# Constant-tile matmuls at the start of TensorE's queue, and a re-annealed plan, in a long-convolution plus linear-attention kernel

## The chip, the core and the metric

The kernel runs on one core of one Trainium2 chip. The time is the device time of one execution, in microseconds (us). Six engines or queues are named: PE (TensorE matmul; PEld is its weight load), DVE (VectorE), ACT (ScalarE), POOL (GpSimd), SP (SyncE, which here only issues DMAs) and the 16 DMA engines. Times in the profile count from the span's start.

## The reference

Two independent blocks over 2048 positions and 576 channels; their outputs stand side by side in the last axis.

```python
def _A_ref(q, k, v, shift_k, ssm_k, ssm_D):
    # k_shift: causal 4-tap convolution of k along S, a weight per channel and tap
    kv = k_shift * v
    # long causal convolution of kv with ssm_k along S, by FFT of length 2S
    y = irfft(rfft(pad(kv)) * rfft(pad(ssm_k)))[:S]
    return q * (y + kv * ssm_D)

def _B_ref(x, wqkv, wo):              # 32 heads of 18 channels
    q, k, v = split(x @ wqkv)
    pq, pk = phi(q), phi(k)           # phi(t) = t+1 if t > 0 else exp(t), plus 1e-6
    kv = einsum("hsd,hse->hde", pk, v); z = pk.sum(s)
    o = einsum("hqd,hde->hqe", pq, kv) / (pq . z + 1e-6)
    return o @ wo
```

## The kernel before

Every piece of work is an operation with a number: `P.op` (and `load` for DMAs) notes what it reads and writes, and gives for each engine that may do it a cost estimate. Nothing is issued there. A long string, `PLAN`, gives the order of issue and the engine of each operation (`P` PE, `A` ACT, `D` DVE, `G` POOL, `S` SP, then the number), and `PLACES` gives each buffer's byte offset in SBUF or its bank in PSUM. Both were made offline by an annealing planner from the estimates. At the end, `order = _issue(P)` reads the plan, and one loop allocates each buffer at its place and calls the operation's function. Each engine takes its operations strictly in the plan's order, waiting for data and for buffers on semaphores. SP issues all DMAs, in the plan's order, into one queue.

The work, by the names used below, with its lines:

- hs: six pieces of `ssm_k` (384 KB each) are loaded, transposed on PE in groups of eight (L480, "htr"), copied from PSUM to hT by ACT or DVE ("hev"), and one row gets `ssm_D` added (L489, "hD").
- Wj: PE spreads the shift weights over all partitions with matmuls that contract over one row (L412), ACT copies them (L415).
- x: `x_sb` holds x by rows. Half of the columns' transposes are done on PE (L343, "xtr", "xtrt"), half by transposing DMAs (L317, L329). Three of these tiles' names are xT, xTt and x_sb.
- k projection (L654, 10 matmuls of 288 columns), exponential on ACT (L659), phi on DVE (L662), 16 times. q projection (L675, 10 matmuls of 512), L679, L682, 10 times, into pqT.
- Convolution taps on DVE (L447 products, L452 and L455 sums), in six pieces; the product with v on DVE or POOL (L458). "Tap 72" below is operation 72, a product of the third piece.
- First transform stage on PE (L510, table Gsb), copied to Ch or Cu; then turned by a transposing DMA (L525) or by DVE (L536); second stage (L554, L561), copied to sph or spu; products p1 and p2 with the filter's spectrum (L595, L592) on DVE or POOL, after a row swap by DMA (X); first inverse stage (L603), copied to Vt; second inverse stage (L628, table Esb), and the product with q (L633).
- Attention: G = x'pk (L708, five groups of 32 matmuls), small products kv, z, den and M, the reciprocal (L795), stored to DRAM and read back spread over partitions (bct), pqT normalised (L838), output matmuls (L851), copies to ob, stores.

The first operations on PE are in the plan before: htr 289, Wj 10, htr 281, htr 287, xtr 46, htr 283, Wj 12, xtr 36, 32, 42, xtrt 34, 48, 38, L510 294 and 296, k 110. SP's first are: hs, cst (the table with the identity), shift weights, hs, x, D, x, x, Gsb, x, Gsb, the two wk loads, then kh (the rows of k), Gsb, kh, kh, the two wq loads, v, kh.

The diff touches the issue loop, a constant tuple beside the plan's other settings, and the two strings.

Of the kernel before, what the change touches and what calls it, by code (L numbers as in the profile page):

```python
# [103 lines left out]
def _issue(P):  # L104

    names = dict(P="PE", A="ACT", D="DVE", G="POOL", S="SP")
    order = []
    for w in PLAN.split():
        o = P.ops[int(w[1:])]
        o.eng = names[w[0]]  # L110
        order.append(o)
    places = [int(w) for w in PLACES.split()]
    for b, p in zip([b for b in P.bufs if b.space != "dram"], places, strict=True):
        b.pos = p
    assert sorted(o.id for o in order) == list(range(len(P.ops)))
    return order
# [99 lines left out]
def kernel(  # L216
# [13 lines left out]
    nc = tc.nc  # L230
# [50 lines left out]
    pqT = SB("pqT", [128, 5, S], side=1, pre=True)  # L281
# [246 lines left out]
    def s2(C, cc, pp, nm, bias):  # L528
        nw = PCH // 2
        g = cc * NPP + pp  # L530
        qt = nm == "u" and g not in UT
        if qt:
# [12 lines left out]
        for kp in range(2):  # L545
# [19 lines left out]
            def ev(e, kp=kp, ps=ps):  # L565
# [3 lines left out]
                else:  # L569
                    copy(e, sp.t[:].rearrange("p (r b) k -> p r b k", r=2)[:, :, 4 * kp:4 * kp + 4],  # L570
                         ps.t.rearrange("p r (b k) -> p r b k", b=4))
            aft = [seq[x] for x in (nm, ("h", g)) if x in seq] if kp == 0 else []
            last = P.op(("PE", T8), mm, rd=[ct, cst], wr=[ps], use=[sp], name="s2" + nm, bias=bias, cnt=8 if qt else 4,
                        after=aft)
# [301 lines left out]

    order = _issue(P)
    psall = nc.alloc_psum_tensor("ps_all", [128, 8, 512], FP32).ap()
    with tc.manual_schedule():
        cnt = 0  # L880
        for o in order:
            for b in o.bufs:
                if b.t is None and b.space != "dram":
                    if b.space == "ps":
                        b.t = psall[:, b.pos:b.pos + b.banks, :]
                    else:
                        cnt += 1
                        b.t = nc.alloc_sbuf_tensor_at("%s_%d" % (b.name, cnt), b.shape, b.dt, offset=b.pos)
            o.fn(o.eng)


T8 = 0.26
UT = (4, 6, 8)
XP = 2
BCD = 1
AFTER = dict(x=8, w=12, q=[3, 7])

PLAN = """
G9 S286 G14 S6 S8 G3 G5 S280 G30 S25 G1 S60 G0 G91 S22 G4 S23 G31 S57 P289 G2 S24 P10 S58 S41 P281 A11 P287 S40
P46 D288 A282 S15 P283 D290 A47 S59 P12 G285 D291 D284 S17 P36 A13 P32 S16 D33 A37 P42 S52 P34 P48 P38 P294 D35  # L900
S53 A49 D39 D43 S21 A295 P296 D297 S50 P110 S56 S28 P44 P298 A111 P101 D112 A299 S55 P92 D61 A45 P98 A93 D62 S54
P119 A99 A102 D94 D100 S18 P122 S20 D63 A120 S19 D64 P125 A123 D103 G65 D124 P107 A126 D121 P116 A108 D127 S51
D109 S321 D66 P292 A117 P128 A293 G29 S315 D67 P104 A129 D118 S300 P113 D130 P152 A114 A105 D115 P95 S305 A153
D68 P155 A96 S310 D106 D69 P161 A156 D97 S356 D72 S350 P158 A162 D154 D157 P137 A159 D163 S26 G70 P149 D160 A138
S27 P140 D139 A150 S7 D151 P322 A141 D71 P324 A323 P146 A325 D142 G326 P303 A147 P301 D73 P131 A304 A302 P134
D74 A132 S398 P316 D148 A135 P318 D133 A317 P308 D75 P143 A309 D136 G320 A319 P311 D77 P306 A144 P164 A307 D145
A312 D76 G185 S186 P333 A165 S189 P167 S399 A334 S188 D166 S187 D78 P327 A168 P329 A328 D169 D79 A330 P391 D82
P331 P170 A332 D80 D81 A392 S345 D83 S340 P387 A171 A172 P385 D84 S335 P182 A386 D85 D87 A388 S411 S412 D86 P389
A183 D88 P176 A390 D89 D184 G90 D393 P194 D177 P394 D195 P396 D406 A395 P196 A397 D178 P351 D197 D198 G400 P179
A352 D199 S210 P432 D180 D355 D419 S211 P173 D181 D401 D433 P438 S228 D174 D175 P479 S222 A439 P357 S224 D480  # L910
P359 S226 A358 P436 S218 G361 D360 A437 P409 S212 P313 D410 P353 S230 A314 P434 S214 D354 D223 P362 S424 A435
S220 P407 D229 A408 S453 P481 D225 A363 P191 G414 D440 S216 A482 P366 S425 D193 D192 A367 D466 P368 P338 A369
D339 P364 D231 A365 P485 P404 D413 A486 S375 P483 D405 A484 P402 S370 D227 P200 A403 P420 P336 D201 A421 S380
P208 D337 P348 A209 P343 P443 A349 D344 P417 S487 A444 P202 D418 P206 A203 P204 S445 A207 P422 S513 D205 P346
A423 P441 D219 P415 A442 P256 D347 G427 A416 P378 S472 A257 P341 S471 D379 P274 A342 S446 S258 D500 P454 S459
A275 P383 P381 A455 D384 P271 A382 D426 P373 P456 A272 P262 D217 A374 S273 S458 A457 P430 D215 A263 P376 P467
D221 S276 A431 P259 S264 D213 A377 P265 A468 S505 D260 P503 G447 S506 A266 P371 P516 A504 D372 P244 A517 S492
P490 P469 S519 A245 D491 P235 S493 S261 D470 P247 S518 A236 S246 D461 S190 P501 A248 P514 P488 S526 D448 A502
P428 S267 A489 P250 D460 S249 A429 D507 P238 S237 A515 D251 P464 A239 S252 D521 P451 S547 A465 P449 D495 P462
D520 A450 P253 A463 D494 P232 A254 D508 A452 P498 D474 A233 P511 S234 D499 S240 P509 A512 D473 P539 P542 D510  # L920
S255 P522 D543 P544 A523 P477 D545 P475 S546 D478 P537 A476 D540 P524 D538 P527 A525 S541 P529 D528 P496 D530
P534 S531 A497 P532 P554 D533 D535 P548 D555 S536 P268 D549 S556 P551 A269 S270 P557 D552 S550 P277 D558 S553
P241 D278 S559 S279 A242 S243
"""
PLACES = """
228384 226464 226432 218240 220192 33536 16512 143552 212480 206720 148160 149312 188256 167776 16768 52480
103040 35840 42240 1 2 20864 68864 1 0 0 3 1 3 7 2 78080 111232 90752 46336 136832 81152 192000 98944 6 33536 4
33536 2 39936 4 34688 2 39936 4 33536 6 33536 0 41088 6 109184 0 107136 6 109184 2 39936 4 33536 2 34688 0 39936
6 50432 2 39936 2 33536 6 33536 0 107136 6 50432 0 107136 4 33536 2 39936 4 39936 6 33536 206720 20608 6 6 4 4 6
50432 212480 32928 32928 68480 6 0 0 33248 78080 80128 6 6 0 2 4 43168 16512 34208 41120 18560 34976 37024 39072  # L930
32928 78080 2 18816 2 32928 0 21120 4 18816 0 18816 6 34080 4 19968 0 16512 6 32928 2 16512 2 58624 0 17664 6
16512 0 41504 0 40352 2 17664 38144 5 1 16768 6 0 56576 0 4 0 0 124544 107136 4 0 51584 124544 0 6 16512 46336 6
6 46336 4 5 120448 4 5 56192 0 3 3 0 24736 161600 0 6 20640 86272 4 2 103040 36256 4 6 132736 6 0 128640 6 7
128640 0 0 0 3 60288 24704 4 6 78080 28832 6 2 24736 115328 2 4 33536 3 0 0 0 56192 60288 6 2 120448 4 6 64384
60288 6 1 28832 0 4 56192 82176 2 6 140928 6 0 87296 0 3 3 3 145024 90368 2 0 98560 2 4 64384 102656 6 4 111232
6 6 50432 64384 4 4 54528 0 4 149312 0 3 0 3 94464 41504 0 6 59776 4 6 20608 78336 4 6 74240 2 4 107136 119424 2
2 123520 0 4 151360 6 2 2 6 2 6 4 2 143168 0 4 4 6
"""


# [28 lines left out]
```

## Time and profile before

| | |
|---|---|
| median of 8 runs | 177.06 us (176.18 to 177.67) |
| the profiled execution | 177.14 us, of which the span from first to last instruction is 175.3 us |
| PE busy | 157.4 us, 90% of the span, 1588 matmuls |
| PEld busy | 118.0 us |
| DVE busy | 147.7 us, 84%, 143 instructions |
| ACT busy | 111.5 us, 64%, 119 instructions |
| POOL busy | 36.0 us |
| DMA | 37.71 MB, mean 215 GB/s |

[...]The row that the profile calls PEclk is the clock that the throttle granted; whether the matmuls ran at that rate has to be read from their spacing. In the timeline a line gives the start, how long the merged group took, the engine, the line of code, the operation with output and inputs, the count, and in brackets how long the engine had been idle and what ended that.

### The profile page before, as it was taken

What the parts mean: (1) busy time and instruction counts of PE and PEld (TensorE: products, weight loads), DVE (VectorE), ACT (ScalarE), POOL (GpSimd) and SP (SyncE); (2) the same over time, 40 slices, a digit from 0 to 9 for tenths busy, and PEclk for the clock granted to TensorE, in tenths of its full rate; (3) what the DMA queues carried; (4) which work ended last, traced back from release to release, by engine and by line L of the source; (5) the groups of instructions that cost most, each with busy time, mean ns of one, the idle gap of its engine ahead of it and who ended that gap; (6) DMA issues with size and microseconds to landing.
All of it is one profiled execution on the core that took longest, in us unless ns stands there. A gap on an engine that the chain in (4) does not pass through costs nothing.

```text
span 175.3 us, 3813 instructions
## 1 busy us (share of the span) xinstructions
PE 157.4 (90%) x1588; PEld 118.0 (67%) x1588; DVE 147.7 (84%) x143; ACT 111.5 (64%) x119; POOL 36.0 (21%) x28
## 2 busy tenths in 40 slices
PE   0798999999969999699999997789999999999991
PEld 0577776767647766588768866655665679987770
DVE  0034599998999999999999999999898899998780
ACT  2362575576548899766360299999999697734211
POOL 8400003600702020000375005400901700000000
PEclk9999999999999999999999999999999999999999
DMA  6999999999999128079300178999998999954374
GB/s 151 288 325 326 371 342 175 220 380 236 242 274 320 65 52 311 4 137 211 135 0 14 50 245 254 167 209 150 220 246 329 374 324 326 329 156 152 120 238 137
DMA packets 53423, 37.71 MB, mean 215 GB/s; under 512 B 32991, under 2 KB 49501, under 8 KB 52894
## 3 DMA queue, kind: packets, MB, share of 16 engines
q1 hardware_dynamic: 53406, 37.47, 79.6%
q8 instruction: 12, 0.20, 0.5%
q14 instruction: 5, 0.04, 0.1%
HBM read 20.16 MB, written 4.98 MB: 143 GB/s over the span
## 4 chain that ended last, share of the span: by engine, by line
PE 55%; DVE 20%; ACT 15%; issue 4%; DMA 3%; SPq 1%; ACTq 0%; DVEq 0%
PE ps_all L851 12%; PE ps_all L603 8%; DVE m L447 7%; PE ps_all L654 7%; PE ps_all L675 6%; PE ps_all L628 6%; PE ps_all L708 5%; ACT Ch L254 4%; DVE m L452 4%; ACT Cu L254 3%; PE ps_all L510 3%; DMA hs<-in_A_ssm_k_dram 3%; ACT sph L254 3%; DVE pqT L682 3%; PE ps_all L343 3%
## 5 line engine op out<-in xcount | busy, mean ns | idle before, releaser
L447 DVE TENSOR_TENSOR m<-kh,Wj 128x3072 bf16<-128x3072 bf16 x12 | 23.2, 1955 | 0.0
L654 PE MATMUL ps_all<-wk,xT 128*128 128x288 bf16 x128 | 20.3, 290 | 2.1 <-DVE pk L662 1.8
L510 PEld LDWEIGHTS <-Gsb 128*128 128x128 bf16 x240 | 17.4, 102 | 6.4 <-issue 5.2
L851 PE MATMUL ps_all<-M,pqT 126*128 126x288 bf16 (+1 forms) x160 | 21.6, 286 | 0.0
L254 ACT ACTIVATE Cu<-ps_all 128x1536 bf16<-128x1536 f32 x10 | 15.3, 1559 | 9.6 <-PE ps_all L510 9.6
L675 PE MATMUL ps_all<-xT,wq 128*126 128x512 bf16 (+1 forms) x80 | 20.6, 380 | 0.0
L708 PE MATMUL ps_all<-pk,x_sb 128*128 128x288 bf16 (+1 forms) x160 | 20.6, 286 | 0.0
L458 POOL TENSOR_TENSOR v<-m,v 128x1536 bf16<-128x1536 bf16 x3 | 9.3, 3098 | 53.4 <-DVE m L455 53.4
L851 PEld LDWEIGHTS <-pqT 126*128 126x128 bf16 (+1 forms) x160 | 15.0, 97 | 5.8 <-issue 2.1
L675 PEld LDWEIGHTS <-wq 128*126 128x126 bf16 (+1 forms) x100 | 13.0, 131 | 7.8 <-issue 0.3
L708 PEld LDWEIGHTS <-x_sb 128*128 128x128 bf16 x160 | 15.5, 98 | 3.9
L254 ACT ACTIVATE Vt<-ps_all 128x1024 bf16<-128x1024 f32 x13 | 13.4, 1040 | 7.2 <-PE ps_all L603 6.3
L603 PE MATMUL ps_all<-cst,sph 128*128 128x128 bf16 x144 | 17.4, 219 | 0.4 <-ACT Cu L254 0.4
L254 ACT ACTIVATE spu<-ps_all 128x1024 bf16<-128x1024 f32 x15 | 15.3, 1046 | 3.7 <-PE ps_all L554 3.7
L254 ACT ACTIVATE Ch<-ps_all 128x1536 bf16<-128x1536 f32 x11 | 16.3, 1525 | 2.0 <-PE ps_all L510 2.0
L603 PE MATMUL ps_all<-cst,X 128*128 128x128 bf16 x144 | 17.4, 219 | 0.0
L654 PEld LDWEIGHTS <-xT 128*128 128x128 bf16 x128 | 12.6, 99 | 6.6 <-issue 3.1
L659 ACT ACTIVATE ek<-ps_all,neg 128x576 bf16<-128x576 f32 x16 | 11.6, 742 | 8.2 <-PE ps_all L654 8.1
L679 ACT ACTIVATE eq<-ps_all,neg 126x1024 bf16<-126x1024 f32 (+1 forms) x10 | 11.1, 1113 | 8.4 <-PE ps_all L675 8.4
L254 ACT ACTIVATE ob<-ps_all 128x576 bf16<-128x576 f32 x13 | 8.6, 659 | 10.3 <-PE ps_all L851 8.8
L603 PEld LDWEIGHTS <-sph 128*128 128x128 bf16 x144 | 14.0, 98 | 1.3 <-issue 0.9
L603 PEld LDWEIGHTS <-X 128*128 128x128 bf16 x144 | 14.1, 98 | 0.9 <-issue 0.5
(86 smaller groups left out, 295.1 us busy)
## 6 DMA issues: line engine op xcount, KB each, us to landing
X<-sph SPq DMA_DIRECT2D x18, 256.0 KB
hs<-in_A_ssm_k_dram SPq DMA_DIRECT2D x6, 384.0 KB
v<-in_A_v_dram SPq DMA_DIRECT2D x2, 1152.0 KB
out_dram<-ob SPq DMA_DIRECT2D x16, 144.0 KB
bct<-rden_rows SPq DMA_DIRECT2D x8, 252.0 KB
kh<-in_A_k_dram SPq DMA_DIRECT2D x1, 1584.0 KB
q<-in_A_q_dram SPq DMA_DIRECT2D x1, 1280.0 KB
out_dram<-q SPq DMA_DIRECT2D x4, 320.0 KB
```

What stands on the lines that cost most here:

```text
L254: nc.scalar.activation(out=o, in_=i, func=ACTF.Copy)
L447: nc.vector.tensor_tensor(out=m.t[:, i:i + 2], in0=i0, in1=i1, op=ALU.mult)
L458: lambda e: vec(e).tensor_tensor(out=vt.t[:, :, c0:c0 + CC], in0=m.t[:, 0], in1=vt.t[:, :, c0:c0 + CC], op=ALU.mult),
L510: nc.tensor.matmul(ps.t[:, bank, lo - 512 * bank:hi - 512 * bank], lhsT=Gsb.t[:, ri, bg, j, :], rhs=src[:, lo - CC * j:hi - CC * j], start ...
L603: nc.tensor.matmul(ps.t[:, j // 4, 128 * (j % 4):128 * (j % 4) + 128], lhsT=src.t[:, 8 * jp + j, :], rhs=W3(wi), start=(wi == 0), stop=(wi ...
L628: nc.tensor.matmul(o, lhsT=Esb.t[:, b, ri, :], rhs=vt[:, 2 * b + ri], start=(ri == 0), stop=(ri == 1))
L654: nc.tensor.matmul(ps.t[:, hh, 0:HALF], lhsT=xs(t, 128 * r, 128), rhs=wk.t[:, t, HALF * hh:HALF * hh + HALF], start=(t == 0), stop=(t == 4))
L659: P.op(("ACT", _act(576) + 0.085), lambda e: nc.scalar.activation(out=eb.t[:], in_=ps.t[:, :, 0:HALF], func=ACTF.Exp, bias=neg1.t[:]), rd= ...
L675: nc.tensor.matmul(ps.t[0:hn, j, :], lhsT=wq.t[:, t, h0:h0 + hn], rhs=xs(t, 1024 * gp + 512 * j, 512), start=(t == 0), stop=(t == 4))
L679: P.op(("ACT", _act(1024) + 0.09), lambda e: nc.scalar.activation(out=eb.t[0:hn], in_=ps.t[0:hn], func=ACTF.Exp, bias=neg1.t[0:hn, :]), rd ...
L708: nc.tensor.matmul(ps.t[:, hh, 0:n], lhsT=x_sb.t[:, r, FT[t]:FT[t] + 128], rhs=pk.t[:, r, HALF * hh:HALF * hh + n], start=(r == 0), stop=( ...
L851: nc.tensor.matmul(ps.t[:, hh, 0:HALF], lhsT=pqT.t[0:hn, c, 128 * r:128 * r + 128], rhs=M.t[0:hn, c, HALF * hh:HALF * hh + HALF], start=(c ...
```

## The change

Before the first operation a tile that is used much later (pqT) is allocated, and DVE sets 512 of its columns to one. In the issue loop each of the first fourteen PE operations gets constant matmuls ahead of it: the number of columns comes from `SPIN`, in matmuls of 512 and then of 128 columns, all with the constant tile as both operands, written into the first PSUM bank of the operation that follows, which overwrites it (its own first matmul has `start=True`). The first operation gets nine of 512, the eleventh three of 128, the other twelve two of 128 each.

```diff
+    spin = list(SPIN)
     with tc.manual_schedule():
         cnt = 0
+        pqT.t = nc.alloc_sbuf_tensor_at("pqT_0", pqT.shape, pqT.dt, offset=pqT.pos)
+        idle = pqT.t[:, 0, 0:512]
+        nc.vector.memset(idle, 1.0)
         for o in order:
...
+            if o.eng == "PE" and spin:
+
+                ps = [b for b in o.bufs if b.space == "ps"][0]
+                n = spin.pop(0)
+                for w in [512] * (n // 512) + [128] * (n % 512 // 128):
+                    nc.tensor.matmul(ps.t[:, 0, 0:w], lhsT=idle[:, 0:128], rhs=idle[:, 0:w], start=True, stop=True)
             o.fn(o.eng)
...
+SPIN = (9 * 512, 256, 256, 256, 256, 256, 256, 256, 256, 256, 384, 256, 256, 256)
```

`PLAN` and `PLACES` are replaced as a whole. The operations themselves and their cost estimates are the same; what differs is order, engine and place. Their starts:

```diff
 PLAN = """
-G9 S286 G14 S6 S8 G3 G5 S280 G30 S25 G1 S60 G0 G91 S22 G4 S23 G31 S57 P289 G2 S24 P10 S58 S41 P281 A11 P287 S40
-P46 D288 A282 S15 P283 D290 A47 S59 P12 G285 D291 D284 S17 P36 A13 P32 S16 D33 A37 P42 S52 P34 P48 P38 P294 D35
...
+G3 S280 G1 S15 G30 S6 S286 G91 G5 S8 G9 G14 S23 S41 G31 S60 G0 G4 S57 G2 P281 S25 P283 S58 A282 S40 D284 P10 S59
+P287 S17 A11 D285 P36 S16 P289 S24 D37 A288 P12 S53 D290 D291 S22 P46 A13 P48 P38 S52 D49 D47 A39 P294 P296 A295
...
```

On PE the new plan starts with htr 281, htr 283, Wj 10, htr 287, xtr 36, htr 289, Wj 12, xtr 46, xtrt 48, 38, L510 294 and 296, k 110, L510 298, then k 113 and 98, and only then the two remaining x transposes of the first half; six k projections stand ahead of the first q projection, where there were four. On SP the first are hs, a small kh piece, cst, hs, shift weights, x, the small wk load, D, Gsb, x, Gsb, the large wk load. Of the copies and products that two engines can do, DVE has 2 hev, 2 hD and 4 ob copies more, and 3 Vt copies, 1 p2, 1 sph copy, 1 G copy and 2 gcol copies fewer; one copy each of Ch and Cu change places with ACT; POOL has three p2 instead of two, two p1 as before, and two hD fewer. In the middle, two L510 groups of Cu (436, 434) now stand before the second last L708 group, and the p1 and p2 of the first pair (401, 400) are both on POOL.

## The prediction

> **What bounds the kernel now.** I read the table of windows first (us; busy time and instruction count per engine; clock; DMA share; GB/s).
>
> ```profile
> 0.00:5.00 5.00, 0.41 (x6) 0.56 (x7) 0.00 (x0) 1.28 (x1) 4.47 (x14) 1.00 0.63 166
> 5.00:10.00 5.00, 4.21 (x41) 3.28 (x39) 1.13 (x3) 2.27 (x3) 1.79 (x4) 1.00 1.03 293
> 10.00:15.00 5.00, 4.22 (x34) 3.19 (x32) 1.25 (x2) 2.74 (x3) 0.00 (x0) 1.00 1.08 335
> 20.00:40.00 20.00, 20.00 (x138) 14.18 (x136) 18.53 (x17) 12.59 (x14) 3.98 (x2) 1.00 1.08 292
> 60.00:80.00 20.00, 18.06 (x171) 13.62 (x170) 19.75 (x18) 17.18 (x18) 1.08 (x2) 1.00 0.51 135
> 100.00:120.00 20.00, 16.92 (x242) 13.07 (x241) 18.91 (x20) 19.77 (x18) 4.89 (x2) 1.00 0.98 205
> 140.00:160.00 20.00, 20.00 (x271) 16.77 (x269) 19.61 (x19) 13.30 (x16) 0.00 (x0) 1.00 0.88 270
> ```
>
> Columns are PE, PEld, DVE, ACT, POOL. The bound moves: PE at the start and from 120, DVE from 40 to 100, ACT from 100 to 120; DMA is full from 5 to 50. DVE does almost nothing before 20.
>
> Then PE's order of time around 19 us: start, duration, group, count.
>
> ```profile
> 13.99 1.65 PE L343 MATMUL ps_all<-cst,x_sb 128*128 128x128 bf16 x14 [0.78 <-DVE xT L256]
> 15.44 2.77 PE L510 MATMUL ps_all<-hT,Gsb 128*128 128x192 bf16 x20
> 18.49 1.04 PE L654 MATMUL ps_all<-wk,xT 128*128 128x288 bf16 x4 [0.29 <-ACT Ch L254]
> 19.37 0.29 PE L654 MATMUL ps_all<-wk,xTt 128*128 128x288 bf16 x1
> 19.49 0.65 PE L654 MATMUL ps_all<-wk,xT 128*128 128x288 bf16 x4
> 19.98 0.29 PE L654 MATMUL ps_all<-wk,xTt 128*128 128x288 bf16 x1
> 20.11 0.28 PE L343 MATMUL ps_all<-cst,x_sb 128*128 128x128 bf16 x2
> 20.22 0.83 PE L510 MATMUL ps_all<-hT,Gsb 128*128 128x192 bf16 x10
> ```
>
> From group start to group start, four 288-column matmuls take 0.88 us at 18.49 and 0.49 us at 19.49; a 128-column one takes 104 ns at 13.99 and 55 ns at 20.11. TensorE runs at half rate until about 19.3 us, though the clock column says 1.00 everywhere. The chain of waits then shows what this delays:
>
> ```profile
> 24.72 6.47 PE ps_all L675 x30
> ...
> 41.42 1.67 DVE m L452
> ...
> 45.29 4.12 DVE m L447
> ```
>
> PE carries the chain to 40 us, then DVE. DVE's first k result (L662) comes at 21.19 and its first tap (L447) at 21.87, behind that PE work. The tap at 45.29 lasts 4.12 us where its row's mean is 1955 ns:
>
> ```profile
> 44.70 3.09 POOL L458 TENSOR_TENSOR v<-m,v 128x1536 bf16<-128x1536 bf16 x1 [11.37 <-DVE m L455]
> 45.20 4.20 DVE L447 TENSOR_TENSOR m<-kh,Wj 128x3072 bf16<-128x3072 bf16 x1
> ```
>
> It ends 1.6 us after POOL's multiply does: POOL kept it out.
>
> [...] Broken work from 4.6 to 13.99 (idle 0.97 us at 6.3 and 1.1 us at 12.9) didn't release it; nearly unbroken work from 13.99 to 19.3 (one gap, 0.45 us) did.[...]
>
> **The change, part by part.** All against the profiled execution: span 175.3, time 177.14 (1.84 around it), 0.08 above the median of 177.06.
>
> 1. Memset and first nine constant matmuls. DVE's memset of 128x512 has no row of its own; nearest is POOL's 64x1024 at 962 ns. Bounds 0.1 and 1.0 us, I take 0.3; DVE is idle until 8.82. PE waits for it, with its whole queue behind, from about 0.74 to 1.05. A 512-column matmul takes 0.215 us at full clock (four of L675 from 24.56 to 25.42), so 0.43 at half: nine take 3.87 us, to 4.9. First data landed at 4.59 (cst); cst is now third in the queue, 0.4 later, so 5.0. Cost 0 to 0.7 us (slow memset); taken 0. That is 3.9 us of unbroken activity followed by real transposes: I expect full clock at about 6, between 4.5 and 8.
>
> 2. 27 constant matmuls of 128 columns before the next 13 operations: 27 x 0.055 = 1.5 us. They come ahead of an operation's wait for data, so some of it lies in waits; lower bound 0, I take 1.4.
>
> 3. What full clock gives. Before its first L675 group PE does, in the old order, four hs transpose groups (16 matmuls in 1.15, so 0.57 each), two Wj (0.49 each), x transposes (40 x 0.056), three Gsb groups (0.67 each) and four k projections (1.225 each): 2.3+1.0+2.2+2.0+4.9 = 12.4 us of full-rate work. It took 24.56 - 4.59 = 20.0, so 7.6 us go to half rate and waits. The new order has the same set plus two k projections, 14.9. From 4.9: 14.9 + 1.4 + 0.6 (1.2 us still at half rate) = 21.8. Level in work that is 24.56 + 2.45 - 21.8 = 5.2 us ahead. Small waits for evictions: 0.4. Lead 4.8.
>
> 4. Is the data there? The queue up to wk held 3205 KB (two hs of 384, cst 120, four x of 288, two Gsb of 256, wk 648, small ones); the new one holds two x fewer and one 17 KB piece more, 2647. With the windows' 166, 293 and 335 GB/s that lands at 11.2 instead of 12.9. The first k projection stands behind 5.7 + 1.3 + 0.6 us of PE work: 12.5 instead of 18.49. wq, v and the first big kh load have the same loads ahead of them as before, so they don't come sooner; wq (some 4.7 us of transfers behind wk and its old followers, 18.7) is before PE's 21.8. SP's later order (transposes of x, second kh pieces, turns, hs) is nearly the same; the loads hs350 and hs356 now wait behind tap 82 on SP with the rden store behind them: hidden if tap 82 ends near 70, since the store's data comes at about 90.
>
> 5. DVE. First k result about 14.5 instead of 21.19, but q results are limited by PE. Following the new order: L682 three times to 31, taps 66 and 67 to 35.7, tap 72 after q157 at 42.2, held by POOL's multiply (41.1 to 44.2), ends 45.9, against 49.4, with one q result (1.2) more done: 4.7 ahead. DVE is the bound to 86, so the 4.7 carries. In numbers the plan gives DVE 2 hT copies, 2 hD and 4 ob copies more, and 3 Vt, 1 p2, 1 Gev, 1 sph and 2 gcol fewer: 1.1+0.4+3.0-3.7-1.2-0.8-1.2-0.3 = -2.7 us. ACT's share rises 1.1, POOL's by one 4.07 multiply less two small hD.
>
> 6. The middle. ACT now idles 8.46 us before 99.56, behind two L708 groups of 3.95, and is then full to 120, where PE loses 3.1 us. The new order puts two Cu groups ahead of the first of those L708 groups: about 6 us idle. Worth 0 to 2.5; taken 0.6, since DVE, which it doesn't feed, is nearly full too. Work from q155 to the end is the same list on PE (120.1 us), and the tail (output, store, 3.8 us after PE) is alike: 0.
>
> Sum: -4.8 - 0.6 = -5.4: 177.14 - 5.4 = 171.7; the 0.08 to the median is noise.
>
> **Rivals.**
> - Late clock:[...] full clock comes only near 12. Against: activity runs on after the nine.[...] Seven us at half rate cost 3.5 and the waits shrink a little: lead 2.5, 174.6.
> - Hidden anyway: landing times of kh and x transposes (DMA full to 50) or ACT's full stretch take it back; for: DMA share 1.03 to 1.10; against: tap 72's data had landed well before it ran. 177.
> - Slower:[...] POOL has five p1/p2 multiplies (21.3 us) instead of four, two in a row. If timing slips so that a two-input DVE operation (p1, p2, L838) meets a 4.53 and a 4.07 one at its start, DVE, full to the end, loses 8.6; it decides from 5.4 on. 177.1 - 5.4 + 8.6 = 180.3. For: the 2.5 us at 45.20 that the old plan lost this way; against: no other such hit in its four.
>
> **How the numbers follow.** Forecast 0.64, late clock 0.16, hidden 0.05, slower 0.15. The forecast alone spans 169.5 to 173.5 (memset 0.7 up, the middle's 2 down). The range takes in the late clock: 169.5 to 176.2. 0.3%, 0.5 us, is what a measurement can tell from none. Faster 0.80, same 0.05, slower 0.15.
>
> **What would show it.** 128-column transposes at 56 ns from about 6; first L654 near 12.5, first L662 near 14.5, first L675 near 22; tap 72 done near 46; ACT's gap before 99 down to 6. Wrong if 104 ns steps persist past 10, if DVE gaps open before 86, or two-input DVE operations last 3 us or more beside POOL.

## The result, and the profile after

The changed kernel takes 175.2 us (median of 19 runs, 174.82 to 177.32) against 176.72 us for the kernel before, run beside it (54 runs). The ratio is 0.9922, with a 95% interval of 0.9903 to 0.994: 0.8% less time, about 1.4 us. Medians and ranges, here and below, are of all runs of a version; ratios are of those within 1.5% of its fastest, and none is given where only one run is left. The forecast was 5.4 us. The profiled execution took 175.04 us, its span is 173.3 us, and the granted clock is 0.99, where the one before had 177.14, 175.3 and 1.00.

The windows view of the changed kernel, with the columns of the same view before (PE, PEld, DVE, ACT, POOL; clock; DMA share; GB/s; "..." marks lines left out):

```profile
0.00:5.00 5.00, 3.54 (x9) 1.34 (x10) 0.48 (x1) 1.28 (x1) 4.47 (x12) 1.00 0.60 144
5.00:10.00 5.00, 5.00 (x59) 3.63 (x58) 1.59 (x4) 2.64 (x3) 1.44 (x4) 1.00 0.89 256
10.00:15.00 5.00, 4.82 (x57) 3.67 (x56) 2.12 (x5) 3.00 (x3) 0.00 (x0) 1.00 1.11 355
...
120.00:140.00 20.00, 17.08 (x185) 10.93 (x184) 18.57 (x15) 13.51 (x17) 12.11 (x3) 0.91 0.87 299
...
134.00:136.00 2.00, 0.53 (x8) 0.12 (x7) 2.00 (x3) 0.00 (x0) 0.00 (x0) 0.88 1.02 316
136.00:138.00 2.00, 2.00 (x28) 1.75 (x20) 1.68 (x2) 1.02 (x1) 0.00 (x0) 0.50 0.84 291
```

Two things are new. The start is filled: PE is busy for 4.8 us or more of each 5 after the first window. And between 120 and 140 PE is busy for 17.08 us of 20, with a granted clock of 0.91 and of 0.50 between 136 and 138. The timeline of the changed kernel shows both places; a line is start, duration of the group, engine, line, operation, and in brackets the idle time ahead:

```profile
1.46 4.02 PE L898 MATMUL ps_all<-pqT 128*128 128x512 bf16 x9 [1.46 <-DVE pqT L884]
...
6.68 1.18 PE L412 MATMUL ps_all<-srow,ones 1*128 1x288 bf16 x4
...
14.14 0.65 PE L654 MATMUL ps_all<-wk,xT 128*128 128x288 bf16 x4
...
23.38 1.03 PE L675 MATMUL ps_all<-xT,wq 128*126 128x512 bf16 x4
...
128.48 4.06 POOL L592 TENSOR_TENSOR X<-spu,X 128x2048 bf16<-128x2048 bf16 x1
129.34 4.28 DVE L595 TENSOR_TENSOR sph<-spu,sph 128x2048 bf16<-128x2048 bf16 x1
134.68 0.75 DVE L256 CAST ob<-ps_all 128x576 bf16<-128x576 f32 x1
135.47 0.63 PE L554 MATMUL ps_all<-ct,cst 32*32 32x512 bf16 x8 [2.84 <-DVE ob L256]
```

The start works: the first k projection (L654) stands at 14.14 instead of 18.49, the first q projection at 23.38 instead of 24.56 with two k projections more done. The lead then lasts and grows. Counting each kind of matmul at its own full-rate step, PE has done by 132.4 us what it had done by about 138.9 before, which is 6.5 us ahead. Within the next ten microseconds most of it goes. POOL runs three multiplies back to back from 120.4 to 132.5. The DVE multiply at 129.34 meets the third one and takes 4.28 us, where the same kind of multiply takes 1.22 at 93.46. The copy to ob behind it on DVE is late, the PSUM bank that it would free is late, and PE stands idle for 2.84 us. Then TensorE runs its next matmuls (L603) at 105 ns from start to start instead of 56, until 138.9. Between 1.7 and 2.0 us of lead are left at the end.

The chain of waits of the changed kernel names the same two places (start, duration, what):

```profile
4.93 6.32 DMA x_sb<-in_B_x_dram
...
129.41 4.20 DVE sph L595
133.62 1.13 DVE X L592
136.10 1.82 PE ps_all L603 x16
```

### The profile page after: what moved, and what is told of

It is laid out like the page before. It is cut to its first block, busy times and chain, and to the rows that moved or that the text cites. A ratio compares the mean times of both kernels' runs of the same rounds, so it can differ in the third digit from the quotient of the medians.

```text
span 173.3 us, 3883 instructions
## 1 busy us (share of the span) xinstructions
PE 159.7 (92%) x1624; PEld 117.7 (68%) x1624; DVE 148.6 (86%) x144; ACT 112.8 (65%) x120; POOL 37.6 (22%) x27
## 4 chain that ended last, share of the span: by engine, by line
PE 63%; DVE 20%; ACT 6%; DMA 6%; issue 3%; SPq 0%; ACTq 0%
PE ps_all L708 11%; PE ps_all L675 10%; PE ps_all L654 9%; PE ps_all L603 8%; PE ps_all L851 7%; DVE pqT L838 6%; PE ps_all L628 6%; PE ps_all L510 4%; DMA x_sb<-in_B_x_dram 4%; DVE sph L595 2%; PE ps_all L561 2%; DMA hs<-in_A_ssm_k_dram 2%; DVE m L447 2%; DVE sph L256 2%; ACT spu L254 2%
## 5 line engine op out<-in xcount | busy, mean ns | idle before, releaser
L654 PE MATMUL ps_all<-wk,xT 128*128 128x288 bf16 x128 | 20.0, 286 | 1.4 <-DVE pk L662 1.4
L708 PE MATMUL ps_all<-pk,x_sb 128*128 128x288 bf16 (+1 forms) x160 | 20.6, 286 | 0.0
L254 ACT ACTIVATE Cu<-ps_all 128x1536 bf16<-128x1536 f32 x11 | 16.5, 1542 | 6.2 <-PE ps_all L510 6.2
L510 PEld LDWEIGHTS <-Gsb 128*128 128x128 bf16 x240 | 16.0, 98 | 6.0 <-issue 4.5
L254 ACT ACTIVATE Vt<-ps_all 128x1024 bf16<-128x1024 f32 x16 | 16.0, 1035 | 6.1 <-PE ps_all L603 5.0
L603 PE MATMUL ps_all<-cst,sph 128*128 128x128 bf16 x144 | 18.3, 225 | 0.3 <-ACT Cu L254 0.2
L708 PEld LDWEIGHTS <-x_sb 128*128 128x128 bf16 x160 | 15.5, 98 | 4.1 <-issue 0.2
L603 PE MATMUL ps_all<-cst,X 128*128 128x128 bf16 x144 | 18.3, 225 | 0.0
L458 POOL TENSOR_TENSOR v<-m,v 128x1536 bf16<-128x1536 bf16 x3 | 9.3, 3102 | 41.0 <-DVE m L455 41.0
L592 POOL TENSOR_TENSOR X<-spu,X 128x2048 bf16<-128x2048 bf16 x3 | 12.2, 4067 | 18.3 <-ACT spu L254 18.3
L654 PEld LDWEIGHTS <-xT 128*128 128x128 bf16 x128 | 12.2, 98 | 5.3 <-issue 2.1
L603 PEld LDWEIGHTS <-X 128*128 128x128 bf16 x144 | 14.6, 101 | 1.1 <-issue 0.7
L603 PEld LDWEIGHTS <-sph 128*128 128x128 bf16 x144 | 14.5, 101 | 1.2 <-issue 0.9
L254 ACT ACTIVATE Ch<-ps_all 128x1536 bf16<-128x1536 f32 x10 | 14.9, 1514 | 0.5 <-PE ps_all L510 0.5
```

Of the source, the lines that this page charges most:

```text
L254: nc.scalar.activation(out=o, in_=i, func=ACTF.Copy)
L510: nc.tensor.matmul(ps.t[:, bank, lo - 512 * bank:hi - 512 * bank], lhsT=Gsb.t[:, ri, bg, j, :], rhs=src[:, lo - CC * j:hi - CC * j], start ...
L592: lambda e: vec(e).tensor_tensor(out=xb.t[:], in0=su.t[:], in1=xb.t[:], op=ALU.mult),
L603: nc.tensor.matmul(ps.t[:, j // 4, 128 * (j % 4):128 * (j % 4) + 128], lhsT=src.t[:, 8 * jp + j, :], rhs=W3(wi), start=(wi == 0), stop=(wi ...
L654: nc.tensor.matmul(ps.t[:, hh, 0:HALF], lhsT=xs(t, 128 * r, 128), rhs=wk.t[:, t, HALF * hh:HALF * hh + HALF], start=(t == 0), stop=(t == 4))
L708: nc.tensor.matmul(ps.t[:, hh, 0:n], lhsT=x_sb.t[:, r, FT[t]:FT[t] + 128], rhs=pk.t[:, r, HALF * hh:HALF * hh + n], start=(r == 0), stop=( ...
```

## The experiments

The theory (A) after this result: the new start and plan are worth the 5.4 us that were forecast, and one collision of a POOL multiply with a DVE multiply gives back most of it, about 3 us by the wait and 1.5 by the fall to half clock behind it. The main rival: the lead of the start is lost to the plan itself (data, ACT or DVE being full), and the collision only fills time that would be lost anyway.

### One multiply moved: e3_p2_on_dve

The third multiply of POOL's row, operation 460, goes to DVE, next to operation 461. All else is the changed kernel.

```diff
-... D236 G460 S506 ... P467 D461 ...
+... D236 S506 ... P467 D460 D461 ...
```

> The whole change, with one multiply (operation 460, L592) moved from POOL to DVE, just ahead of the product that follows it there (461). Theory A, that 4.5 us of the lead were lost because this multiply kept DVE's L595 out for 3.1 us, PE then stood 2.84 us and fell to half clock: L595 at about 129 takes 1.2 us, the gap and the half clock near 136 are gone, 171 to 172.5 us. Rival B, that DVE and PE are full there anyhow and something else comes late at once: 174.5 to 175.5 us.

Measured: 171.6 us (6 runs, 171.23 to 173.75), ratio to the kernel before 0.9727 (0.9673 to 0.9782). The same place in its timeline:

```profile
129.54 1.18 DVE L595 TENSOR_TENSOR sph<-spu,sph 128x2048 bf16<-128x2048 bf16 x1
130.64 1.21 DVE L592 TENSOR_TENSOR X<-spu,X 128x2048 bf16<-128x2048 bf16 x1
131.78 0.75 DVE L256 CAST ob<-ps_all 128x576 bf16<-128x576 f32 x1
132.23 0.86 PE L554 MATMUL ps_all<-ct,cst 32*32 32x512 bf16 x24
```

The multiply takes 1.18 us, the copy to ob comes 2.9 us earlier, PE has no gap, and TensorE keeps its clock (1.00 from 120 to 140, where the changed kernel has 0.91). DVE got 1.2 us of work more and the kernel became about 3.5 us faster than the changed one. Theory A holds for the wait and the half clock together: one placed multiply was worth more than everything the change brought.

### The half clock behind the gap: e6_keep_clock

Sixteen constant matmuls fill PE's 2.84 us of idle time; the collision stays.

```diff
+            if o.id == 271:
+                free = [b for b in o.bufs if b.space == "ps"][0]
+            if o.id == 469:
+                for w in range(16):
+                    nc.tensor.matmul(free.t[:, 0, 0:384], lhsT=cst.t[:, 352:480], rhs=cst.t[:, 0:384], start=True, stop=True)
```

> The changed kernel with sixteen more constant matmuls (128x384) ahead of the L554 group that stood idle for 2.84 us at 132.6; GpSimd's multiplies stay where they are, so VectorE is still held. Theory A (the fall to half clock at 136 is a cost of its own, about 1.5 us, on top of the wait): granted clock 1.00 at 136 to 138, and 173.3 to 174.0. Rival (only the wait costs, and the half clock behind it is hidden under VectorE): no change, about 175.

Measured: 175.69 us (6 runs, 174.31 to 177.19), ratio 0.9884 (0.984 to 0.9928). The median is the rival's. The windows and the timeline of its profiled execution say something else:

```profile
5.00:10.00 5.00, 4.64 (x47) 3.76 (x47) 0.79 (x3) 2.64 (x3) 1.43 (x4) 0.77 1.00 272
...
136.00:138.00 2.00, 2.00 (x31) 1.19 (x29) 2.00 (x3) 1.02 (x1) 0.00 (x0) 1.00 0.91 211
```

The clock at 136 to 138 is 1.00 instead of 0.50. DVE's operations run 0.9 us later than in the changed kernel ahead of that place and 0.6 us earlier behind it, so 1.5 us were gained there, as expected. The 0.9 us were lost at the start, where this execution fell back to half clock (0.77 from 5 to 10), and another 1.3 us after the last store was issued (3.7 us to the end of the span instead of 2.4; I have no cause for it). The two runs with a clock of 1.00 throughout took 174.31 and 174.43 us, under every run of the changed kernel. So the half clock is a cost of its own in the trace. As a time it is 0.4 to 0.9 us, between these two runs and the lowest and the median run of the changed kernel, not the 1.2 to 1.9 that I expected; and its size stays open, since the intervals of the two ratios overlap and the kernel before read 177.29 us beside this version, against 176.72 beside the changed one.

### The other collision: e5_tapv_on_dve

In the changed kernel, tap 72 is still held by POOL's product of the same stretch (operation 70, L458). This kernel is e3 with operation 70 on DVE.

```diff
-... A159 G70 D145 ...
+... A159 D70 D145 ...
```

> As e3 (the product of operation 460 on VectorE), and the tap product of piece 2 that GpSimd made (operation 70, L458, 1.9 us) goes to VectorE too, beside its neighbours. Theory A (GpSimd's multiply also holds VectorE's tap chain by about its own length, and VectorE bounds that stretch): the operation that waited behind it takes its plain time of about 1.75 us instead of 3.6, and the time is 170.5 to 171.0, about 0.9 under e3. Rival (what VectorE gains by not being held it spends on the extra product, or the stretch is bounded elsewhere): as e3, 171.3 to 171.9.

The tap in the timeline of e3, and then of this kernel:

```profile
43.34 3.62 DVE L447 TENSOR_TENSOR m<-kh,Wj 128x3072 bf16<-128x3072 bf16 x1
```

```profile
43.21 1.75 DVE L447 TENSOR_TENSOR m<-kh,Wj 128x3072 bf16<-128x3072 bf16 x1
...
46.68 0.95 DVE L458 TENSOR_TENSOR v<-m,v 128x1536 bf16<-128x1536 bf16 x1
```

The tap takes 1.75 us, the product costs DVE 0.95 (POOL's took 3.1), and from 47 us to the end everything runs 0.9 to 1.4 us earlier: span 169.1 against 170.0. The times split: three runs at 170.53 to 171.0, three at 172.37 to 172.5 with a mean clock of 0.987 to 0.99, median 171.68, ratio 0.968 (0.9637 to 0.9723). The trace is theory A's; the median is the rival's, and the three runs that make it so show a loss of clock that the profiled execution (171.0 us, clock 1.00) doesn't have.

### The parts of the change: plan alone, matmuls alone, and the two kinds of them

e1_plan_only has the new plan with `SPIN = ()`; e2_spin_only the old plan with the constant matmuls.

> The new plan without any constant matmul (the memset stays). Theory A, that the early full clock is what the lead is made of: matmuls run at half rate until about 16 us, the first k projection comes near 16 to 17 us, the lead at the first q projection falls from 3.6 us to about 1, and the run takes 177 to 178.5 us, no faster than the kernel before. Rival B, that the re-annealed order gives the gain and the constant matmuls little: 174.5 to 175.5 us.

> The old plan and places with the constant matmuls. Theory A: full clock near 6 us, the lead at the first q projection is about 3 us, and since the old plan has no long POOL multiply meeting a DVE two-input operation in its last third, the lead reaches the end: 173 to 174.5 us, faster than the whole change. Rival B: 176 to 177 us, the old order doesn't use the lead.

The plan alone: 178.18 us (22 runs, 172.38 to 179.75), the median 1.006 of the kernel before. The start of its profiled execution (176.97 us) is better than theory A had it:

```profile
14.91 1.06 PE L654 MATMUL ps_all<-wk,xT 128*128 128x288 bf16 x4
...
24.45 0.81 PE L675 MATMUL ps_all<-xT,wq 128*126 128x512 bf16 x3
```

The half rate ends at about 15.8 us, where it ended at 19.3 in the kernel before, without one constant matmul. The first q projection at 24.45, with two k projections (2.45 us) more done, is a lead of 2.6 us, not of 1. In e2's trace the first q projection stands at 22.36, a lead of 2.2; both together have 3.6. So the parts overlap, and each alone gives more than half of the early lead.

Further on, e1 has the same collision (a DVE multiply of 5.07 us beside POOL's row) and a PE gap of 3.6 us, after which nothing of its lead is left. One of its runs, the only one with a clock of 1.00, took 172.38; it was not profiled and I can't explain it. The matmuls alone: 176.79 us (15 runs, 174.88 to 178.4), where theory A had 173 to 174.5. The ratio of 0.9925 (0.9885 to 0.9965) rests on eight of the fifteen runs; the median of all is 0.9986 of the 177.04 beside it, so whether the matmuls alone bring the 0.8% is not settled. As times, neither part is shown to be worth more than both together, and what the plan could add is lost at the collision. The plan without constant matmuls, but with operation 460 moved as in e3, was not run: how much of e3's gain needs the constant matmuls is open.

In the trace of e2 the lead is 2.2 us from the first q projection to 70 us, and then about 1 to the end. Its timeline at that place, and below it that of the kernel before:

```profile
68.76 0.83 PE L510 MATMUL ps_all<-v,Gsb 128*128 128x192 bf16 x10 [1.26 <-DMA wv<-in_B_wqkv_dram]
70.17 1.30 PE L510 MATMUL ps_all<-hT,Gsb 128*128 128x192 bf16 x10 [0.59 <-ACT Ch L254]
71.27 5.33 PE L708 MATMUL ps_all<-pk,x_sb 128*128 128x288 bf16 x32
```

```profile
70.96 0.82 PE L510 MATMUL ps_all<-v,Gsb 128*128 128x192 bf16 x10 [1.26 <-ACT Ch L254]
72.37 0.83 PE L510 MATMUL ps_all<-hT,Gsb 128*128 128x192 bf16 x10 [0.59 <-ACT Ch L254]
73.03 4.11 PE L708 MATMUL ps_all<-pk,x_sb 128*128 128x288 bf16 x32
```

Two gaps of 1.26 and 0.59 us, 0.8 apart, and the 32 matmuls behind them take 5.33 us, at a clock of 0.59 from 70 to 72 and 0.56 from 72 to 74, where the kernel before needs 4.11. The kernel before has the same two gaps and kept its clock over them in this execution (1.00 from 66 to 76); but of its 52 runs beside e2, 23 have a clock of 0.985 to 0.987, so such a split is there without the constant matmuls too. Half clock followed the gap of 2.84 us in the changed kernel as well (0.50 from 136 to 138). I tested whether the two gaps of e2 are the cause with e9_old_keep, e2 with three constant matmuls in the second gap:

```diff
+            if o.id == 167:
+                free = [b for b in o.bufs if b.space == "ps"][0]
+            if o.id == 331:
+                for w in range(3):
+                    nc.tensor.matmul(free.t[:, 0, 0:384], lhsT=cst.t[:, 352:480], rhs=cst.t[:, 0:384], start=True, stop=True)
```

> The old plan with the constant matmuls at the start (as e2), and three constant matmuls (128x384) in the second of the two idle times at 67.5 to 70.2, into a PSUM bank that is free by then. Theory A (these two idle times close together are what takes TensorE to half speed in some runs, and splits e2 into runs near 175.0 and runs of 176.2 to 178.4): all runs with a mean clock of 0.995 or more, and 174.9 to 175.3. Rival (the first idle time of 1.26 alone does it, or the split has another cause): runs with a clock of 0.985 to 0.987 remain, and the median is near 176.8.

Measured: 175.66 us (6 runs, 174.83 to 177.47), ratio 0.9934 (0.9888 to 0.9979). Five of six runs have a clock of 0.996 or more, where e2 had five of fifteen; in the profiled one the L708 group takes 4.11 us again. That agrees with the cause, on few runs. But three of the five took 175.48 to 177.03 at that clock, so the clock is not all of e2's spread; the rest stays open.

e4_first_only keeps only the nine long matmuls (`SPIN = (9*512,)`), e7_between_only only the 27 short ones (the first entry 0).

> The whole change with only the nine 512-column matmuls, none between the following operations. Theory A, that the first nine and the real work behind them are enough: full clock near 6 us, up to 1.5 us less PE work at the start, 174 to 175.2 us. Rival B, that the small ones are needed to keep the activity up: 104 ns steps of 128-column matmuls until 10 us or later, 176 us or more.

> The changed kernel without the nine long constant matmuls ahead of the first operation; the twenty-seven short ones between the first operations stay. Theory A[...]: full speed only from 10 us or later, and 176.5 or more. Rival (the short ones and the real work are enough): full speed before 10 us, about 175.2.

e4: 177.91 us (22 runs, 175.77 to 179.48), ratio 1.0012 (0.9983 to 1.0041), no gain over the kernel before. Its first q projection comes at 24.48, where e1's came at 24.45, so at the start the nine alone add nothing to the plan. Not all of its time is the start's: in its late collision PE is idle for 3.60 us, against 2.84 in the changed kernel. e7: 181.31 us (6 runs, five from 179.85 to 181.62 and one of 176.95 us), and its steps fall to the full-rate 56 ns only at about 17 us, as theory A says. That is read from an execution of 181.48 us, which loses time later too (clock 0.83 from 140 to 160), so its median is more than the price of the start, and with one run 3 us under all the others the price isn't settled. The windows of e4 at the start:

```profile
5.00:10.00 5.00, 5.00 (x50) 3.31 (x48) 2.01 (x5) 2.64 (x3) 1.43 (x4) 0.89 0.89 250
...
8.00:9.00 1.00, 1.00 (x20) 1.00 (x18) 0.43 (x2) 1.00 (x2) 0.00 (x0) 0.97 0.85 277
9.00:10.00 1.00, 1.00 (x7) 0.40 (x5) 0.97 (x3) 0.46 (x1) 0.00 (x0) 0.50 0.88 248
...
10.00:15.00 5.00, 4.20 (x35) 3.78 (x34) 0.99 (x2) 2.61 (x3) 0.00 (x0) 0.50 1.10 346
15.00:20.00 5.00, 5.00 (x47) 4.06 (x46) 4.16 (x4) 3.29 (x5) 0.00 (x0) 0.92 1.08 383
```

Full speed was reached before 6 us (the eight x transposes at 8.06 step by 56 ns) and lost again just before 9 (a clock of 0.50 from 9 to 10), with PE busy all the time; the wait of 0.8 us for x_sb begins only at 10.3, so it isn't the cause. The one-row products and the narrow transposes stand there without short matmuls between them; whether that is the cause was not tested. That the short ones are needed at the start, the rival's view, agrees (0.50 from 10 to 15, where the changed kernel with them has 1.00); the place of the loss was not foreseen.

### The one-row products: e8_wj_contiguous and e10_best

L412 starts a matmul every 256 ns in the changed kernel, as it did before at half clock. It reads every fourth element of one row. e8 reads them side by side, which leaves out the right order: Wj holds other weights.

```diff
-rhs=srow.t[0:1, HALF * hh:HALF * hh + HALF, j]
+rhs=srow.t[0:1].rearrange("p d j -> p (d j)")[:, D * j + HALF * hh:D * j + HALF * hh + HALF]
```

> The changed kernel with L412's moving operand (one row of 288) read side by side instead of at every fourth element; Wj then holds other weights, all other work is as it was. Theory A (the stride sets the pace): steps of about 123 ns instead of 256, and the first k projection about 1 us earlier. Rival (one row of contraction sets it, or float32): steps stay at 256.

One run, 179.21 us, so only its trace is used. The timeline of its start:

```profile
6.55 0.65 PE L412 MATMUL ps_all<-srow,ones 1*128 1x288 bf16 x4 [0.23 <-DMA srow<-in_A_shift_k_dram]
...
11.10 0.77 PE L343 MATMUL ps_all<-cst,x_sb 128*128 128x128 bf16 x8 [1.10 <-DMA x_sb<-in_B_x_dram]
11.66 0.42 PE L898 MATMUL ps_all<-pqT 128*128 128x128 bf16 x2
```

Four take 0.65 us instead of 1.18, steps of 123 ns: the stride sets the pace, as theory A says. But the first k projection comes 1.2 us later (15.36), not 1 us earlier. The x transposes now wait 1.10 us for x_sb, and behind that wait 128-column matmuls step by 105 ns again. The changed kernel waits 0.3 us for the same transfer at 11.3: its start is bound by data, and L412's slow steps filled time that it would have waited anyway.

e10_best uses this: e5 with L412 reading side by side (the copy on ACT, whose edit is not shown, puts the channels in order) and the freed time given to constant matmuls ahead of the waits.

```diff
-rhs=srow.t[0:1, HALF * hh:HALF * hh + HALF, j]
+rhs=srow.t[0:1, HALF * hh + 72 * j:HALF * hh + 72 * j + 72, :]
...
-SPIN = (9 * 512, 256, 256, 256, 256, 256, 256, 256, 256, 256, 384, 256, 256, 256)
+SPIN = (9 * 512, 256, 512, 256, 256, 256, 256, 4 * 512, 256, 256, 384, 256, 256, 256)
```

> As e5, with L412's moving operand read side by side (ACT's copy puts the channels back in order) and the time that this frees filled with constant matmuls: 512 columns ahead of the first Wj and 2048 ahead of the x transposes that waited for x_sb. Theory A (the start is bound by the landing of x_sb at 11.1, and waits there take TensorE back to half speed in some runs): the first k projection stays at 13.9 to 14.2, all runs have a clock of 0.995 or more, and 170.4 to 171.0. Rival (the runs of e5 near 172.4 lose their time elsewhere): the split remains, median near 171.7.

Measured: 170.97 us (6 runs, 170.56 to 171.29), ratio 0.9669 (0.9638 to 0.97), every clock 0.995 or more. The first k projection stands at 13.56, 0.3 earlier than I expected, since x_sb was there by 10.73 in this execution. None of the six runs stands near 172.4, as three of e5's six did, and the version is the fastest here, 3.3% under the kernel before. That agrees with theory A, on few runs; the constant matmuls without the new reading of L412 were not run, so which of the two ended the split is not shown.

## Why the prediction was wrong, by its own steps

The forecast of 171.7 is what e3 takes (171.6), so the sum left out the collision and little else in total. That it came so near is in part luck: the early lead was 1.2 us too high in it, and what comes later too low.

- **The step that failed** is the dismissal in the third rival ("no other such hit in its four"), and with it step 5, which put POOL's extra multiply into POOL's share and priced it at nothing for DVE. That POOL can keep DVE out was named, from the tap of 4.20 us, and so was this sign of being wrong (a two-input DVE operation of 3 us or more beside POOL). Its place was half seen: the prediction counted two multiplies in a row, and there are three. DVE was kept out once, not twice: 3.1 us on its multiply, passed on as a PE gap of 2.84 us, and about 1.5 us of half clock behind it, which the rival had no term for. Together they make up most of the 4.7 us or so that PE's lead loses between 132 and 142. The rival's own 180.3 was too high, because it took two full POOL durations for what was the remainder of one. The same multiply took 4.28 us, ending 1.1 us after POOL's, and 1.18 with only POOL's neighbour moved (e3).
- **Steps 1 and 2**, the constant matmuls: nearly right. The first starts at 1.46 instead of 1.05, since DVE's memset takes 0.48 us and ends later; full-rate steps come at 5.8, against "about 6". The trace of the kernel before had shown half rate through the broken work up to 13.99 and full rate only at 19.3, behind 5.3 us of nearly unbroken work; that the nine (3.9 us) and the first transposes would be enough was an estimate. Here full rate came 4.3 us after the first matmul (1.46 to 5.8). The late clock of the first rival did not come true in the profile after. In e6's start something like it did: full clock was there before 5 us and lost again before 10 (the 0.77 above), with no idle time of PE over 0.24 us between its first matmul and that loss.
- **Step 3**, the lead: 4.8 forecast, 3.6 measured at the first q projection. The term that was off in the sum is Wj, put at 0.49 us each at full clock; it is 1.1 at either clock, which makes 1.2 us for two. But Wj is not what bounded the start: in e10, where it is fast (0.65 us for the four matmuls instead of 1.18), the first q projection comes at 22.80, 0.6 us earlier, and x_sb was there 0.6 us earlier too. The step also put the whole lead down to full clock and had no term for the new order, which alone gives 2.6 us (e1).
- **Step 4** looked at wk, which was there, and not at x_sb, which wasn't. Even a fast Wj could not have brought the first k projection to 12.5: e8, e10 and the chain of the changed kernel show x_sb there at 10.7 to 11.3, with 2.8 us of PE work between it and the k projection.
- **Step 5**, DVE: tap 72 ended at 46.8 instead of 45.9, still held by POOL's product (3.63 us instead of 1.75), as foreseen; the lead after it was 3.8 instead of 4.7, which is step 3's shortfall.
- **Step 6**, the middle: ACT's idle time ahead of its Cu copies is 6.2 us in all, against 9.6 before; the one gap that the forecast took from 8.46 to about 6 us is 4.05, ending at 96.62. The lead grew from about 4.9 at DVE's reciprocal to 6.5 on PE at 132, so this part was worth some 1.6, inside the 0 to 2.5 given, where I took 0.6. With the 1.1 us gained between tap 72 and the reciprocal, which no step had, it made up for step 3.

The rival of a late clock (174.6) is near the measured time by accident: TensorE was at full rate from 5.8.

## What to carry to other kernels

When an order puts several GpSimd multiplies in a row, list the two-input DVE operations that stand beside them and price each at the remainder of the multiply (here 3.1 us for the L595 at 129.34 and 1.9 for tap 72), plus what waits behind DVE. Beside the same multiplies DVE's copies from PSUM (L256, 1.22 us at 121.72) and transposes (L536, 1.23 at 125.92) took no longer than elsewhere (1.21 at 117.64, 1.25 at 99.72). A lead won early is only worth what the later stretch with the least slack lets through, so price that stretch before the start. Constant matmuls kept TensorE's clock in a later wait of 2.84 us too (e6: 1.00 from 136 to 138 instead of 0.50); read from the trace whether the clock fell there at all before placing them.

## What the runs showed that I had not expected

- Short gaps were followed by half rate on TensorE: 2.84 us in the changed kernel (0.50 from 136 to 138), 1.26 and 0.59 us close together in e2 (0.59 and 0.56 from 70 to 74), 1.10 us in e8 (0.66 from 10 to 15). Not each time: the changed kernel has gaps of 1.26 and 0.55 us at 67 to 68 us too, and kept its clock over them (1.00 from 66 to 76), as the kernel before did over 1.35 us at 48.8 (the k projections behind it, from 50.12, step by 123 ns). And e4 lost it just before 9 us with PE busy throughout, so in these runs the length of a gap alone does not tell. The half clock then lasted 3.4 us in the changed kernel (135.5 to 138.9) and 6.9 us in e4 (8.9 to 15.8).
- The one-row moving operand of 288 elements with a stride of four elements (L412) stepped by 256 ns at full clock (the changed kernel) and at half (the kernel before); side by side (e8) it stepped by 123.
- With the new plan, the nine long constant matmuls without the 27 short ones (1.5 us of work) bring nothing at the start (first q projection at 24.48, against 24.45 without any); with them it comes at 23.38.
- The new order alone, without a constant matmul, has full rate at about 15.8 us instead of 19.3.
